# Gated linear attention and a cosine-gated MLP in one kernel: another form of the first two pairs' scores, and a new order of loads and steps

## The chip, the cores and the metric

One core of a Trainium2 chip. The metric is the device time of one execution in microseconds, the median of the runs that are shown.

## The reference

Attention with a decaying state for 4 batches, 8 heads, 768 tokens, head size 48, and then an MLP on the tokens:

```python
for t in range(S):
    state = alpha[:, :, t, :, None] * state + k_t[:, :, :, None] * v_t[:, :, None, :]
    y[:, :, t] = einsum('bhd,bhde->bhe', q[:, :, t], state)
x = y.transpose(0, 2, 1, 3).reshape(B * S, H * D)      # 3072 x 384
h = x @ w_in                                           # 384 x 2048
out = (h * cos(h)) @ w_out                             # 2048 x 384, float32
```

## The kernel before, in words

The tokens are worked on in twelve *pairs* J = 0 to 11 of 256 tokens, three pairs to a batch. A pair lies on 128 partitions with two tokens each (e = 0 for the even, 1 for the odd token) and is made of two chunks c of 64 partitions, 128 tokens each. For each pair there are these steps, each a small function:

- `load` (L107) brings a (alpha), k, q and v of a pair with one DMA each, 384 KB, on SP's queue. `load_w1` (L125) and `load_w2` (L131) bring quarters of the two weights with a cast to bf16 on GpSimd's queue, four of each.
- `ln` (L144) takes the logarithm of alpha on ScalarE; `cums0` and `cums` (L191, L173) sum the logarithms along the tokens with products against triangular matrices; for pairs from 3 on GpSimd first multiplies the two tokens' alphas (`mula`, L152) and VectorE subtracts (`sub`, L197). `icp` and `exps` (L206, L213) take exponentials on ScalarE; from pair 3 on they come together with the next logarithm as one `session` (L223, called "eb" in the plan). The exponential and the sine need different tables of ScalarE, which `act_set` (L139) and the activation load when they change.
- `scale_k`, `scale_q` (L231, L236; "sk", "sq") multiply k and q by the exponentials, on GpSimd or VectorE as the plan says. `cast_v` (L241) casts v on GpSimd.
- `trans` (L283) transposes k and q with TensorE and `evict_T` (L302) copies the result out; from pair 8 on a DMA does it (`trans_dma`).
- `scores` (L308) makes the products of k and q of a chunk, 128 x 128 for each head, 8 matmuls for each c. Its rows are the keys of the whole chunk (both tokens), its columns the queries. `mask` (L317) multiplies them by a triangular mask on VectorE.
- The v that meets these scores must have the chunk's 128 keys on 128 partitions. `stack_v` (L244; "vst") brings it there with four DMAs, and for pairs 0 to 2 `stack_v_pe` (L253; "vpe") does it with products against an identity, and `evict_vs` ("vev") copies the result out on ScalarE.
- `outer` (L324), `add_state` and `decay_state` (L351) carry the state from chunk to chunk; `decay` makes its factor. `yT` (L358) makes the output of the attention, transposed: from the state and q (12 or 24 matmuls), and from v and the masked scores (32 matmuls); `evict_y` (L386) copies it out to `xT`.
- `mlp1` (L396; "m1 u") makes a quarter of the first stage for a pair, 12 matmuls of 256 columns; `cosine` (L405) takes the cosine on ScalarE, as a sine with a shift; `gate` (L410) multiplies on VectorE. `mlp2` (L420; "m2 c part") makes a quarter of the second stage for 128 tokens, 4 matmuls of 384 columns; `evict_o` and `store` bring the result out.

Products into PSUM share three buffers of two banks each (tag "h": sums of the first pairs, transposes, scores, state products, y, first stage); a new one waits until the oldest user is copied out.

The order of all this is written out by hand: `PLAN` (L476) has for each step a row with one number for each pair, and the steps are issued in the order of these numbers, each engine working its instructions off in that order (":D" and ":A" behind a number put a step on VectorE or ScalarE). `IDLE` (L546) puts products of zeros, whose result nobody reads (`idle`, L454), between the steps. `GATES` (L99) holds loads back: a load that it names waits on SP until the last matmul of the step named there is done (`pass_gate`, L102). Before the change, the loads of pair 3 and a of pair 4 wait for the first pair's m2, c = 0, part 3; in the plan that stands after the loads of pair 2's a and q, which are not held back.

## Time and profile before

| | |
|---|---|
| median of 3 runs | 183.55 us (183.15 to 183.85) |
| the profiled execution | 183.31 us |
| its span, first to last instruction | 181.5 us |
| TensorE busy | 172.4 us (95%) |
| VectorE busy | 129.4 us (71%) |
| ScalarE busy | 123.9 us (68%) |
| GpSimd busy | 82.5 us (45%) |
| HBM read and written | 25.17 and 4.72 MB |
| granted TensorE clock | 1.00 |

PE is TensorE, PEld its weight loads, DVE VectorE, ACT ScalarE, POOL GpSimd; SPq and POOLq are DMA issues of SP and GpSimd. A row of a timeline has the start and the length in us, the engine, the line, the operation, result and sources, how many in a row, and in brackets how long the engine stood idle before it and who ended that. A strip has 40 digits, one for each 4.54 us, in tenths of busy time. In the DMA rows q1 is the queue of SP's loads and q0 that of GpSimd's weights: packets, MB, and the time of the packets as a share of 16 engines (above 100% where packets overlap).

### The profile page before, as it was taken

How to read it: one execution, taken by the hardware profiler on the slowest of the kernel's cores; microseconds unless marked ns; L12 is line 12 of the kernel's file. 1: busy time of each engine (PE TensorE's matmuls, PEld its weight loads, DVE VectorE, ACT ScalarE, POOL GpSimd, SP SyncE). 2: the span in 40 equal slices, each digit the busy share in tenths (PEclk: the TensorE clock that was granted, in tenths of full speed). 3: DMA queues.
4: the chain of work that ended last, by engine and by line, in shares of the span. 5: the costliest groups of instructions: out<-in, count | busy, mean ns of one | idle time of the engine just before them, and what ended most of it. 6: DMA issues, size and time to landing. Idle time of an engine off the chain costs nothing.

```text
span 181.5 us, 5505 instructions
## 1 busy us (share of the span) xinstructions
PE 172.4 (95%) x2339; PEld 123.6 (68%) x2342; DVE 129.4 (71%) x174; ACT 123.9 (68%) x159; POOL 82.5 (45%) x115
## 2 busy tenths in 40 slices
PE   7898789899999999999999999999999999999993
PEld 2444668665786767866786787778667767766672
DVE  7057976299989779699879898786877873535520
ACT  2765758988798999985688988937497704363201
POOL 6289770437486465959980495409025310000000
PEclk9999999999999999999999999999999999999999
DMA  5999999999969959984994998961669761030222
GB/s 143 261 261 250 153 192 202 247 251 269 236 151 285 263 123 297 276 214 105 298 180 79 269 121 219 185 144 33 131 147 262 89 154 68 2 130 4 87 87 87
DMA packets 68840, 31.55 MB, mean 174 GB/s; under 512 B 59728, under 2 KB 68816, under 8 KB 68816
## 3 DMA queue, kind: packets, MB, share of 16 engines
q1 hardware_dynamic: 64960, 27.96, 68.4%
q0 software_dynamic: 3712, 3.15, 11.6%
q8 instruction: 18, 0.29, 0.7%
q10 hardware_dynamic: 144, 0.10, 0.2%
q14 instruction: 6, 0.05, 0.1%
HBM read 25.17 MB, written 4.72 MB: 165 GB/s over the span
## 4 chain that ended last, share of the span: by engine, by line
PE 70%; DMA 9%; ACT 5%; POOL 4%; SPq 3%; issue 3%; DVE 3%; ACTq 0%
PE o_ps L431 28%; PE h_ps L401 28%; DMA w<-in_moe_w_out_dram 6%; PE y_ps L381 5%; SPq L110 3%; DMA v<-in_v_dram 3%; PE A_ps L314 3%; PE U_ps L332 2%; PE o_last L431 1%; DVE A_sb L320 1%; ACT L141 1%; POOL un L354 1%; POOL w L132 1%; PE T_ps L290 1%; ACT lna L146 1%
## 5 line engine op out<-in xcount | busy, mean ns | idle before, releaser
L413 DVE TENSOR_TENSOR gsb<-h_ps,c_sb 128x1024 bf16<-128x1024 f32 x48 | 57.9, 1222 | 23.0 <-ACT c_sb L408 22.1
L401 PE MATMUL h_ps<-xT,w 128*128 128x256 bf16 x576 | 68.5, 273 | 1.3 <-DVE A_sb L320 0.8
L431 PE MATMUL o_ps<-w,gsb 128*128 128x384 bf16 x368 | 67.0, 326 | 0.8 <-DMA w<-in_moe_w_out_dram 0.8
L408 ACT ACTIVATE c_sb<-h_ps,halfpi 128x1024 bf16<-128x1024 f32 x48 | 52.8, 1114 | 20.8 <-PE h_ps L401 20.6
L401 PEld LDWEIGHTS <-w 128*128 128x128 bf16 x576 | 55.2, 98 | 11.3 <-DMA w<-in_moe_w_in_dram 1.9
L431 PEld LDWEIGHTS <-gsb 128*128 128x128 bf16 x400 | 37.0, 98 | 21.9 <-issue 1.4
L320 DVE TENSOR_TENSOR A_sb<-A_ps,msk 128x1024 bf16<-128x1024 f32 x24 | 29.0, 1218 | 4.4 <-PE A_ps L314 4.2
L354 POOL TENSOR_TENSOR un<-us,c 128x384 bf16<-128x384 f32 x20 | 16.8, 838 | 31.5 <-DVE us L346 24.3
L233 POOL TENSOR_TENSOR kh<-k,icp 128x384 bf16<-128x384 f32 x19 | 19.7, 1038 | 9.1 <-ACT icp L209 5.2
L238 POOL TENSOR_TENSOR qh<-q,cp 128x384 bf16<-128x384 f32 x17 | 17.2, 1024 | 13.0 <-ACT cp L219 10.0
L390 ACT CAST xT<-y_ps 128x384 bf16<-128x384 f32 x12 | 6.7, 594 | 11.4 <-PE y_ps L381 11.3
L444 ACT COPY o_sb<-o_ps 128x384 f32<-128x384 f32 x12 | 5.7, 479 | 11.3 <-PE o_ps L431 11.3
L242 POOL CAST vp<-v 128x768 bf16<-128x768 f32 x12 | 10.1, 845 | 6.0 <-DMA v<-in_v_dram 5.7
L146 ACT ACTIVATE lna<-a 128x768 bf16<-128x768 f32 x12 | 10.1, 843 | 3.2 <-DMA a<-in_alpha_dram 3.2
L458 PE MATMUL idle_ps<-zeros 128*128 128x512 bf16 x38 | 10.8, 426 | 1.5 <-DVE halfpi L77 1.2
L141 ACT ACT_TABLE_LOAD x9 | 11.5, 1283 | 0.9 <-PEq L576 0.7
L408 ACT ACT_TABLE_LOAD x9 | 11.5, 1283 | 0.2
L154 POOL TENSOR_TENSOR a<-a 128x384 f32<-128x384 f32 x9 | 9.0, 1001 | 5.6 <-DMA a<-in_alpha_dram 5.6
L346 DVE TENSOR_TENSOR us<-U_ps,un 128x384 f32<-128x384 f32 x16 | 8.8, 551 | 2.6 <-PE U_ps L332 1.3
L444 DVE COPY o_sb<-o_ps 128x384 f32<-128x384 f32 x11 | 6.1, 555 | 4.8 <-PE o_ps L431 4.7
L314 PE MATMUL A_ps<-qkT 48*128 48x128 bf16 x192 | 8.8, 217 | 0.3 <-issue 0.3
L390 DVE CAST xT<-y_ps 128x384 bf16<-128x384 f32 x12 | 6.6, 586 | 2.1 <-PE y_ps L381 1.9
(68 smaller groups left out, 144.0 us busy)
## 6 DMA issues: line engine op xcount, KB each, us to landing
a<-in_alpha_dram SPq DMA_DIRECT2D x12, 384.0 KB, 5.8
k<-in_k_dram SPq DMA_DIRECT2D x12, 384.0 KB, 5.8
q<-in_q_dram SPq DMA_DIRECT2D x12, 384.0 KB, 6.0
v<-in_v_dram SPq DMA_DIRECT2D x12, 384.0 KB, 5.3
out_dram<-o_sb SPq DMA_DIRECT2D x23, 192.0 KB, 2.2
vs<-vp SPq DMA_DIRECT2D x36, 64.0 KB, 3.1
w<-in_moe_w_in_dram POOLq DMA_DIRECT2D x4, 384.0 KB, 7.0
w<-in_moe_w_out_dram POOLq DMA_DIRECT2D x4, 384.0 KB, 8.6
```

The lines of the kernel that those rows point to most:

```text
L141: nc.scalar.preload_act_table_set("natural_log_exp_and_others")
L146: nc.scalar.activation(out=lna_t[J % NL][:, :, :, 0:D].rearrange("p e h d -> p h e d"), in_=a_sb.pop(J), func=AF.Ln)
L233: eng.tensor_tensor(out=kh_t[J % NQ][:, :, e, :, 0:D], in0=kqv["k", J][:, :, e].rearrange("p (n a) d -> p n a d", a=2), in1=icp_.rearrange ...
L238: eng.tensor_tensor(out=qh_t[J % NQ][:, :, e, :, 0:D], in0=kqv["q", J][:, :, e].rearrange("p (n a) d -> p n a d", a=2), in1=cp.rearrange(" ...
L314: last = nc.tensor.matmul(A_ps[J, c][:, a, p, :], qkT[r, c, NP + p, :], qkT[r, c, p, :], start=True, stop=True)
L320: nc.vector.tensor_tensor(out=A_sb[J][:, c].rearrange("s a p t -> s (a p) t"), in0=A_ps.pop((J, c)).rearrange("s a p t -> s (a p) t"), in1 ...
L354: nc.gpsimd.tensor_tensor(out=u, in0=U_sum.pop(n), in1=c2_sb[J][:, :, c].unsqueeze(3).to_broadcast([C, NP, 2, D]), op=ALU.mult)
L390: ins = copy(out=xT[J][:, :, c * C : (c + 1) * C].rearrange("r i (t e) -> r i e t", e=2), in_=y_ps[J][:, c, 0 : KT * C].rearrange("r (i e ...
L401: last = nc.tensor.matmul(h_ps[J, u][:, f, :], w1[:, kk, ft * C : (ft + 1) * C], xT[J][:, kk, :], start=(kk == 0), stop=(kk == KT - 1))
L408: nc.scalar.activation(out=c_sb[J, u], in_=h_ps[J, u], func=AF.Sin, bias=halfpi, scale=1.0)
L413: nc.vector.tensor_tensor(out=gsb[J][:, u * FW : (u + 1) * FW], in0=h_ps.pop((J, u)), in1=c_sb.pop((J, u)), op=ALU.mult)
L431: last = nc.tensor.matmul(o[:, 0 : cols.stop - cols.start], gsb[J][:, ft, c * C : (c + 1) * C], w2[:, ft, cols], start=(done == 1 and ft = ...
```

## The change

- **Scores by parity of the key, for pairs 0 and 1** (`ALT`). The scores of a pair are split by the key's token e instead of by chunk: each product gives 64 rows, the keys of one token of one chunk, and the two chunks lie below each other on the partitions. 16 matmuls for each e instead of 8 for each c. Their rows lie as v lies anyway, so `yT` takes v unstacked, with 64 matmuls of 64 rows instead of 32 of 128. A mask `msk2` of its own is made at the start with eight more copies on VectorE.
- The unstacking of v for pairs 0 and 1 (steps "vpe" and "vev") is gone.
- **Gate:** a, k, q and v of pair 2 wait for the second quarter of pair 1's first stage ("m1 1", u = 1); the loads of pairs 3 and 4 are no longer held back.
- **Plan:** a new order of all steps. At the start: a, k, q, v of pair 0, then a, v, k, q of pair 1 (before: both a first, and q and a of pair 2 directly behind pair 1). The four w1 loads stand directly behind the first steps of pair 0. All scalings of q, and two of three of k, of pairs 0 and 1 go to VectorE. 27 idle products instead of 41.
- `WSPAN`, through which a weight load could cover several quarters, is empty, so each load covers one quarter as before.

```diff
+    ALT = (0, 1)
+    msk2 = consts.tile([C, 2, 2, HC], BF, tag="msk2")
+    for c in range(2):
+        r = slice(HC * c, HC * c + HC)
+        for e in range(2):
+            for e2 in range(2):
+                nc.vector.tensor_copy(out=msk2[r, e, e2], in_=(triu if e <= e2 else striu)[r, r])
...
-    GATES, AFTER = {('a', 3): ('m2', 0, 0, 3), ('k', 3): ('m2', 0, 0, 3), ('q', 3): ('m2', 0, 0, 3), ('v', 3): ('m2', 0, 0, 3), ('a', 4): ('m2', 0, 0, 3)}, {}
+    GATES, AFTER = {('a', 2): ('m1', 1, 1), ('k', 2): ('m1', 1, 1), ('q', 2): ('m1', 1, 1), ('v', 2): ('m1', 1, 1)}, {}
...
+    def scores_alt(J, e):
+        qkT = qkT_sb[J]
+        A_ps[J, e] = ps.tile([C, 2, NP, C], FP, tag="h", name="A_ps", bufs=3)
+        for p in range(NP):
+            for c in range(2):
+                for a in range(2):
+                    r = slice(64 * a, 64 * a + D)
+                    last = nc.tensor.matmul(A_ps[J, e][HC * c : HC * c + HC, a, p, :], qkT[r, c, NP + p, HC * e : HC * e + HC],
+                                            qkT[r, c, p, :], start=True, stop=True)
+        pass_gate(("scores", J, e), last)
...
-            in1=msk.rearrange("s e2 t -> s (e2 t)").unsqueeze(1).to_broadcast([C, H, C]), op=ALU.mult)
+            in1=(msk2[:, c] if J in ALT else msk).rearrange("s e2 t -> s (e2 t)").unsqueeze(1).to_broadcast([C, H, C]), op=ALU.mult)
...
+            for half, e, c in [(z // 4, z // 2 % 2, z % 2) for z in range(8)] if J in ALT else [(z % 2, 0, z // 2) for z in range(4)]:
...
+                        if J in ALT:
+                            r = slice(HC * c, HC * c + HC)
+                            todo.append((c, g, i, vp_t[J % NV][r, e].rearrange("s h d -> s (h d)")[:, m], A[r, e, a, p, :]))
```

The plan, for pairs 0 to 3 of the rows that the prediction speaks of (a smaller number is issued earlier):

```diff
-        "load a": "20 10 630 980 ...    "load k": "110 240 1160 1450 ...
-        "load q": "140 390 490 1530 ... "load v": "150 340 1200 1560 ...
-        "w1": "480 380 580 560 ...      "w2": "1080 1010 1090 860 ...
-        "ln": "50 30 640 1250 ...       "trans": "230 500 1270 1590 ...
-        "m1 0": "780 990 ...  "m1 1": "720 1130 ...  "m1 2": "840 930 ...  "m1 3": "810 1040 ...
-    IDLE = [(35, 10), (55, 3), (225, 9), (265, 5), (315, 6), (405, 4), (495, 3), (605, 1)]
+        "load a": "10 150 950 1100 ...  "load k": "50 310 990 1470 ...
+        "load q": "80 350 1130 1500 ... "load v": "120 190 1290 1650 ...
+        "w1": "300 270 370 410 ...      "w2": "980 630 940 840 ...
+        "ln": "20 320 960 1150 ...      "trans": "170 550 1260 1560 ...
+        "m1 0": "690 810 ...  "m1 1": "590 790 ...  "m1 2": "860 890 ...  "m1 3": "750 920 ...
+    IDLE = [(25, 10), (165, 8), (205, 1), (245, 1), (325, 1), (455, 6)]
```

In the new order the steps between the loads of pair 1 and the third pair's logarithm are: scores and mask of pair 0, y of pair 0 with both copies out on ScalarE, state products and transposes of pair 1, first quarter product (pair 0, u = 1), scores and masks of pair 1, second (0, 0), y of pair 1, third (0, 3), fourth (1, 1), then (1, 0), (0, 2), (1, 2), (1, 3), the second stage of pair 0, and sums, scalings and transposes of pair 2.

## The prediction, made before the changed kernel ran

> **What bounds the kernel now.** I read the strip of the span first, then the chain that ended last, then the timelines of the engines up to 50 us, then the DMA queues by window.

> ```profile
> PE   7898789899999999999999999999999999999993
> ```

> A digit is 4.54 us. From the eleventh digit on (45 us) TensorE is full to the end, so nothing after that can be gained except by less work for it. Before that it has holes, partly filled with idle products (L458).

> ```profile
> 25.55 10.58 DMA w<-in_moe_w_out_dram
> ...
> 41.65 0.32 PE cums L168
> ...
> 67.55 0.45 PE U_ps L332 x16
> 68.00 0.47 PE T_ps L290 x32
> 68.46 2.06 PE o_ps L431 x12
> 70.52 0.90 PE y_ps L381 x56
> ```

> The chain (start, us, what) runs through the weights' DMA until 36 us; after the sums of the fourth pair (41.65 + 0.32 = 41.97) it is almost only TensorE. I take **41.97 us as the mark**: by then TensorE has done all eight first-stage products of the first two pairs, the first pair's second stage, the third pair's sums and transposes and the fourth pair's sums. When the changed kernel has done the same set, the same work is left, and the time changes by the shift of the mark, plus what is given back behind it.

> ```profile
> 21.14 1.47 PE L401 MATMUL h_ps<-xT,w 128*128 128x256 bf16 x12 [0.75 <-DVE A_sb L320]
> ...
> 36.82 1.47 PE L401 MATMUL h_ps<-xT,w 128*128 128x256 bf16 x12
> ```

> The eight products of 12 matmuls run from 21.14 to 38.1; one takes 1.31 us (1.47 with its latency of 0.16). Back to back they would take 10.5 us, not 17. They wait for weights, for scores and for each other's buffers. That is the room for a gain: about 6 us at most.

> **The change part by part.** *Inputs.* The order on SP becomes a, k, q, v of pair 0, then a, v, k, q of pair 1.

> ```profile
> 4.53 0.84 ACT L146 ACTIVATE lna<-a 128x768 bf16<-128x768 f32 x1 [2.51 <-DMA a<-in_alpha_dram]
> 6.04 0.84 ACT L146 ACTIVATE lna<-a 128x768 bf16<-128x768 f32 x1 [0.66 <-DMA a<-in_alpha_dram]
> ```
> ```profile
> 13.59 0.82 POOL L242 CAST vp<-v 128x768 bf16<-128x768 f32 x1 [0.25 <-DMA v<-in_v_dram]
> 14.35 0.93 POOL L126 DMA_DIRECT2D w<-in_moe_w_in_dram  x1
> ```

> The first load lands at 4.53, the second at 6.04, the seventh (this v) at 13.5: 1.5 us each. So in the new order k of pair 1 (seventh) lands at 13.5 and its q (eighth) at 15.05. Eight loads, not ten, stand ahead of the weights.

> *Weights.* In the program as built the first w1 issue stands on GpSimd behind the cast of v0 and one small decay. v0 (fourth) lands at 9.05, the cast takes 0.8 to 1.1, so the issue is at about 10.4 instead of 14.35; the other three follow one state update, from 12.2 to 14.6. Do they slow k and q of pair 1, still under way? The two queues, packets, MB and share, in the windows 16.5 to 17.0, 17.5 to 18.0, 21.5 to 22.0 and 33.8 to 34.0:

> ```profile
> q1 hardware_dynamic: 322, 0.12, 111.2%
> q0 software_dynamic: 9, 0.01, 10.9%
> ...
> q0 software_dynamic: 92, 0.09, 113.1%
> q1 hardware_dynamic: 20, 0.01, 8.0%
> ...
> q0 software_dynamic: 31, 0.03, 101.1%
> ...
> q0 software_dynamic: 41, 0.03, 97.7%
> q1 hardware_dynamic: 40, 0.02, 28.3%
> ```

> The first weight, issued at 14.35, moves almost nothing until the inputs (q1) are through at 17; then it has the engines to itself. I read that as: what came first is finished first. Then q of pair 1 is undisturbed, and the weights begin at 14.3 instead of 17. The last window, inputs arriving as the last weights end, shows equal packet counts; that is rival A. A w1 load has 384 packets, at 92 in half a microsecond 2.1 us; four end by 23 (27 before), four w2 loads by about 31 (36.13 before).

> *The first two pairs.* Unstacking v takes two groups of products and two ScalarE casts away; scores by parity double the score matmuls (16 to 32 a pair) and the v part of y (32 to 64). At 0.90/56 = 16 ns each that is 96 x 16 = 1.5 us more for TensorE, bounded by nothing (if it fills holes) and 1.5; it lies before the mark, where TensorE waits anyway, and I count only what stands in the chain below. The eight mask copies added on VectorE fall before 6 us, when it has nothing to do until the first exponentials; price nothing.

> *The chain in the new order.* VectorE now scales q and k of pair 1, all three behind the mask of pair 0. Rows of VectorE:

> ```profile
> 16.32 1.02 DVE L238 TENSOR_TENSOR qh<-q,cp 128x384 bf16<-128x384 f32 x2
> ...
> 35.22 3.49 DVE L413 TENSOR_TENSOR gsb<-h_ps,c_sb 128x1024 bf16<-128x1024 f32 x3 [4.16 <-ACT c_sb L408]
> ...
> 40.91 1.28 DVE L305 COPY qkT<-T_ps 128x1024 bf16<-128x1024 bf16 x2
> ...
> 43.01 0.56 DVE L346 TENSOR_TENSOR us<-U_ps,un 128x384 f32<-128x384 f32 x1 [0.29 <-PE A_ps L314]
> 43.48 1.22 DVE L320 TENSOR_TENSOR A_sb<-A_ps,msk 128x1024 bf16<-128x1024 f32 x1
> 44.61 0.95 DVE L233 TENSOR_TENSOR kh<-k,icp 128x384 bf16<-128x384 f32 x1
> ```

> - k at 13.5, its scaling 0.55 and the mask 1.2: 15.3, when q is there.
> - three scalings: 0.51 each (16.32 row) to 0.95 (44.61 row), 1.5 to 2.85; I take 2.0, since a cast and a state update run on GpSimd beside the first two: 17.3.
> - outer product 0.45 and transposes 0.47 with latency: 18.3. The first product of the first stage follows at once (21.14 before).
> - two evictions, both on VectorE now, 1.28, and a state sum 0.55: 20.15; the first mask 1.2: **21.35**. In the built program the second product waits for exactly this mask, which frees its bank.
> - that product 1.31; y of pair 1 with 24 + 64 matmuls at 16 ns 1.4; a third product 1.31: 25.4. The fourth is the gate of the third pair's inputs: it ends at 26.7. Then four more at 1.31 (VectorE's gates go by 3.49/3 = 1.16, so TensorE sets the pace): **31.95**.

> ```profile
> 31.50 0.87 ACT L219 ACTIVATE cp<-cums_h 128x392 f32<-128x392 f32 x2
> ...
> 38.33 1.11 ACT L408 ACTIVATE c_sb<-h_ps,halfpi 128x1024 bf16<-128x1024 f32 x1 [0.76 <-PE h_ps L401]
> 39.46 1.28 ACT L141 ACT_TABLE_LOAD   x1
> 40.76 0.84 ACT L146 ACTIVATE lna<-a 128x768 bf16<-128x768 f32 x1
> ```

> - last sine 0.15 + 1.11, table load 1.28, logarithm 0.84: 35.35; sums 0.5 (one is 0.32), four exponentials at 0.44: 37.6; four scalings at 0.51 on VectorE (bound 0.95): 39.65; transposes 0.45: **40.1**. Before, the third pair's logarithm ran under the first products; now it stands behind the last sine and this stretch is exposed. TensorE has the second stage of pair 0 beside it, 32 matmuls at 2.06/12: 5.5 us, and the sums, and waits about 1.

> *The gate.* The waiting load stands on SP, and everything later on SP waits behind it, so the third pair's a starts at 26.8 at the earliest. It finds the weights still under way and lands when they are through, at 32 to 33.5; k, a of pair 3, q and v follow at 1.5. a is needed at 34.5 and q at 37.6, so the gate costs nothing; without that cover it would cost what is late at the logarithm. The traffic up to the fifth pair's a is the same set of loads in both programs.

> **Sum.** 40.1 - 41.97 = -1.9 us. Given back: in the built order the eviction of the third pair's y on ScalarE stands behind the exponentials of pair 4 and a logarithm (four at 0.44 and 0.84, 2.6 us); I find TensorE waiting 0.6 there, between nothing and 1.2. Net **-1.3 us**. The profiled execution took 183.31 us (span 181.5); that gives 182.0. The median of the three runs is 183.55, 0.24 above, so I say **182.1**. The bounds (1.5 to 2.85 for the scalings of pair 1, up to 1.75 more for those of pair 2, 0 to 1.2 given back) reach from 180.9 to 185.2; the upper ends are counted as C and D.

> **Rivals.**

> *A: the queues alternate packet by packet* (slower). From the moment the first weight has descriptors ready, about 12.8, until q of pair 1 is through, each input packet waits for a weight packet. A pair of packets takes 0.5/92 + 0.5/322 us over the engines (first and second window), so the 1024 rows of a load take 7.2 us instead of 1.5 and q lands near 20.7. The three scalings, the transposes and every product behind them stand in TensorE's order, so the chain moves by 5.7 less the 0.25 that q waits for VectorE now: mark 45.5, 187.4 us. It decides if the weights' packets start before 14 us. For it: 41 packets against 40 in the last window. Against: the second window, 92 against 20, and that nothing of the weight moved before 16.5. Chance 0.13.

> *B: the engines alternate by whole transfers.* Then q of pair 1 stands behind one weight, 2.1 us where the weight is ready before k is through (k's packets end near 12.7, the weight is ready at 12.5 to 13), so half of the engines or more; the last engine decides. Mark 41.95, 183.9 us: no change. The two windows fit it as well as the forecast. Chance 0.17.

> [...]

> *C: the exposed stretch is longer.* The weights' queue has a hole in this trace (31 packets in the window from 21.5, a third of 92); if it comes again and moves all loads behind it, or the scalings of pair 2 take 0.95 each as beside GpSimd's work, the third pair's transposes come 1 to 1.75 later: 183.1 to 183.9, no change. Chance 0.15.

> *D: the edit does less than it says:* the early products wait for scores and masks, not for weights, and the order is as long as the old one. The row at 21.14 names the mask, which speaks for it. It needs the chain up to 21.35 to be 2 us longer, by the scalings' upper bound and contention on every VectorE step: 184.0 to 185.3. Chance 0.07.

> **How the numbers follow.** Forecast 0.48, A 0.13, B 0.17, C 0.15, D 0.07. Half a per cent, 0.9 us, is about what a measurement of this kernel can tell from no change. Against the median the bounds of same are 182.6 and 184.5. The forecast case lies below them nine times in ten; B and C fall mostly within; A and D above. Faster 0.46 (with a little of C), same 0.28, slower 0.26 (with a third of B). The range 180.9 to 185.3 takes in all but A, and leaves out about 0.2 with the tails.

> **What would show it.** In the changed profile: q of pair 1 scaled on VectorE from about 15.3 (20 under A, 17 under B); the first products at 18.3 and 21.4; the eighth ending at 32; the third pair's logarithm at 34.5 directly behind a table load; its transposes ending at 40; TensorE full from about 49. Wrong would be: holes of TensorE later than 50 us, which this working takes to be none, or a third pair's a that lands after 34.5, which would make the gate the bound.

## The result and the profile after

| | before | after |
|---|---|---|
| median of 20 runs | 183.66 us (183.15 to 184.57) | 185.61 us (183.64 to 189.47) |
| the profiled execution, its span | 183.31, 181.5 us | 185.62, 183.7 us |
| granted TensorE clock | 1.00 in the profiled execution, 0.997 to 1.00 in all its runs beside the experiments | 0.997 to 1.00 in 9 of the 20 runs, 0.99 in 7, 0.98 in 4 |

The ratio is 1.0052, 95% interval 1.0029 to 1.0075: about half a per cent slower, not 0.8% faster. (It is made from undisturbed runs alone, those within 1.5% of the kernel's fastest, so it is smaller than the ratio of the medians.) The changed kernel also scatters over 6 us, the kernel before over 1.4, and its time goes with the clock: the median of the 9 runs at 0.997 to 1.00 is 184.3 us, of the 7 at 0.99 186.6, of the 4 at 0.98 188.0.

TensorE's strips of the changed kernel, busy time and granted clock, one digit for each 4.59 us:

```profile
PE   7885799889999999999599999999999999999993
...
PEclk9999999999999999999889999999999999999999
```

In the row of before every digit after the tenth was a 9, up to the last. Here the twentieth, 87 to 92 us, is a 5, and the granted clock drops in it and the next. From there to the end the row is as before.

The early chain first, TensorE and then ScalarE and VectorE (start, length, engine, line, operation, how many, and in brackets the idle time before and who ended it):

```profile
18.40 1.48 PE L428 MATMUL h_ps<-xT,w 128*128 128x256 bf16 x12
...
21.67 1.47 PE L428 MATMUL h_ps<-xT,w 128*128 128x256 bf16 x12 [0.87 <-DVE A_sb L344]
...
24.31 8.04 PE L428 MATMUL h_ps<-xT,w 128*128 128x256 bf16 x72
...
40.59 0.41 PE L300 MATMUL T_ps<-ident_bf,qh 64*128 64x64 bf16 x16 [0.69 <-DVE qh L248]
```
```profile
15.68 1.32 DVE L248 TENSOR_TENSOR qh<-q,cp 128x384 bf16<-128x384 f32 x2
16.92 0.55 DVE L243 TENSOR_TENSOR kh<-k,icp 128x384 bf16<-128x384 f32 x1
...
34.81 0.84 ACT L156 ACTIVATE lna<-a 128x768 bf16<-128x768 f32 x1
...
37.90 0.56 DVE L248 TENSOR_TENSOR qh<-q,cp 128x384 bf16<-128x384 f32 x1 [3.15 <-ACT cp L229]
...
38.38 1.04 DVE L243 TENSOR_TENSOR kh<-k,icp 128x384 bf16<-128x384 f32 x2
...
39.34 1.19 DVE L248 TENSOR_TENSOR qh<-q,cp 128x384 bf16<-128x384 f32 x1
```

The third pair's transposes make room for the next product at 40.59 + 0.33 = 40.92, where the prediction had 40.1 and the kernel before needed until 41.97 for the same work. So at the mark the changed kernel is 1.05 us ahead. At the end of the span it is 2.2 behind (183.7 against 181.5). Between lies this *hole*, a stretch in which TensorE stands idle, again in its timeline:

```profile
86.58 0.34 PE L408 MATMUL y_ps<-qkT,un 128*32 128x128 bf16 x12
86.74 0.50 PE L408 MATMUL y_ps<-A_sb,vs 128*32 128x128 bf16 x20
89.18 0.41 PE L408 MATMUL y_ps<-A_sb,vs 128*32 128x128 bf16 x12 [1.94 <-issue]
```

In the middle of y of pair 6, with 12 of its last 32 matmuls left, TensorE stops for 1.94 us. "issue" means that the profile shows nothing that it waits for. The chain of waits and the windows around it (TensorE's busy time is the second number of a window, the granted clock the third from the end) give the rest of the price:

```profile
71.54 4.04 PE h_ps L428 x36
...
87.24 1.94 issue
...
90.67 5.37 PE h_ps L428 x36
```
```profile
86.00:88.00 2.00, 1.24 (x88) 1.07 (x77) 1.41 (x3) 1.41 (x2) 1.67 (x2) 1.00 1.27 270
88.00:90.00 2.00, 0.82 (x28) 0.68 (x27) 0.37 (x1) 0.37 (x1) 2.00 (x4) 1.00 1.21 280
90.00:92.00 2.00, 2.00 (x19) 1.32 (x14) 2.00 (x3) 1.84 (x3) 1.77 (x3) 0.51 1.07 290
92.00:94.00 2.00, 2.00 (x13) 1.52 (x12) 0.54 (x1) 0.71 (x1) 1.16 (x2) 0.64 0.91 230
```

After the hole TensorE is granted half of its clock for 3.4 us (0.50 in the window 90.04 to 93.45; called a half clock below): the two windows lack (0.49 + 0.36) x 2 = 1.7 us of clock, at half rate that is twice as long. The 36 first-stage matmuls in it take 5.37 us, not 4.04. Hole and half clock cost 1.94 + 1.33 = 3.27 us; without them this execution would have taken about 182.3 (an estimate).

**What TensorE waits for.** The profile's page has a queue that moves no data of the kernel:

```profile
PE 171.8 (94%) x2414; PEld 124.1 (68%) x2416; DVE 129.8 (71%) x181; ACT 122.7 (67%) x160; POOL 77.7 (42%) x111
...
q8 instruction: 19, 0.31, 0.7%
```

```profile
q1 hardware_dynamic: 1399, 0.53, 126.4%
...
q1 hardware_dynamic: 1368, 0.52, 121.3%
q8 instruction: 1, 0.02, 3.8%
...
q1 hardware_dynamic: 135, 0.05, 124.7%
q8 instruction: 1, 0.02, 37.6%
```

One block moves from 86.3, for 3.8% of 2 us x 16 engines = 1.2 us, in a time in which the loads (q1) fill all engines. It is through at 87.5, after TensorE stopped (87.24), and TensorE goes on 1.6 us later. From this come two theories:

- **F:** TensorE ran out of instructions. The block came late, behind input loads, and the block in use was eaten quickly, because between 84 and 87 us stand the smallest matmuls of the kernel (transposes, y of two pairs): counted 256 recorded instructions back from the stop, it lasted from 84.1 to 87.2, 3.1 us. That a block is asked for about when the one before it is begun is the author's estimate; the trace shows only when its packet moves, here 2.2 us after that. The change left TensorE's work there as it was; it moved the block boundaries and the loads.
- **V:** TensorE waits there for data, the stacked v of pair 6 before all, whose four DMAs stand on SP between the loads.

### The profile page after: what moved, and what is told of

Read it like the earlier page. It is cut to its first block, busy times and chain, and to the rows that moved or that the text cites. A ratio compares the mean times of both kernels' runs of the same rounds, so it can differ in the third digit from the quotient of the medians.

```text
span 183.7 us, 5670 instructions
## 1 busy us (share of the span) xinstructions
PE 171.8 (94%) x2414; PEld 124.1 (68%) x2416; DVE 129.8 (71%) x181; ACT 122.7 (67%) x160; POOL 77.7 (42%) x111
## 4 chain that ended last, share of the span: by engine, by line
PE 84%; ACT 5%; DVE 4%; issue 2%; DMA 2%; POOL 1%; POOLq 0%
PE h_ps L428 35%; PE o_ps L458 31%; PE y_ps L408 5%; PE A_ps L338 3%; PE U_ps L356 3%; DMA a<-in_alpha_dram 2%; PE T_ps L300 2%; DVE qh L248 2%; PE o_last L458 1%; ACT icp L219 1%; DVE kh L243 1%; DVE A_sb L344 1%; PE cums L178 1%; ACT lna L156 1%; ACT cp L229 1%
## 5 line engine op out<-in xcount | busy, mean ns | idle before, releaser
L458 PE MATMUL o_ps<-w,gsb 128*128 128x384 bf16 x368 | 66.5, 326 | 0.0
L428 PEld LDWEIGHTS <-w 128*128 128x128 bf16 x576 | 56.2, 99 | 10.8 <-issue 1.0
L458 PEld LDWEIGHTS <-gsb 128*128 128x128 bf16 x400 | 36.8, 98 | 20.8
L248 POOL TENSOR_TENSOR qh<-q,cp 128x384 bf16<-128x384 f32 x16 | 15.9, 1004 | 9.8 <-DVE o_sb L471 6.6
L243 POOL TENSOR_TENSOR kh<-k,icp 128x384 bf16<-128x384 f32 x16 | 15.9, 1001 | 7.0 <-ACT icp L219 3.8
L471 ACT COPY o_sb<-o_ps 128x384 f32<-128x384 f32 x14 | 6.7, 477 | 14.5 <-PE o_ps L458 14.5
L417 ACT CAST xT<-y_ps 128x384 bf16<-128x384 f32 x14 | 7.7, 592 | 9.8 <-PE y_ps L408 9.6
L417 DVE CAST xT<-y_ps 128x384 bf16<-128x384 f32 x10 | 5.7, 587 | 5.4 <-PE y_ps L408 5.4
L485 PE MATMUL idle_ps<-zeros 128*128 128x512 bf16 x25 | 8.0, 463 | 1.3 <-DVE halfpi L84 1.2
L408 PE MATMUL y_ps<-A_sb,vs 128*32 128x128 bf16 x320 | 6.5, 219 | 1.9 <-issue 1.9
L248 DVE TENSOR_TENSOR qh<-q,cp 128x384 bf16<-128x384 f32 x8 | 5.6, 733 | 3.7 <-ACT cp L229 3.7
```

Source lines behind the costliest of these rows:

```text
L243: eng.tensor_tensor(out=kh_t[J % NQ][:, :, e, :, 0:D], in0=kqv["k", J][:, :, e].rearrange("p (n a) d -> p n a d", a=2), in1=icp_.rearrange ...
L248: eng.tensor_tensor(out=qh_t[J % NQ][:, :, e, :, 0:D], in0=kqv["q", J][:, :, e].rearrange("p (n a) d -> p n a d", a=2), in1=cp.rearrange(" ...
L408: last = nc.tensor.matmul(y_ps[J][32 * g : 32 * g + 32, c, i * C : (i + 1) * C], l, r, start=(c, g) not in begun, stop=(c, g, i) not in ou ...
L417: ins = copy(out=xT[J][:, :, c * C : (c + 1) * C].rearrange("r i (t e) -> r i e t", e=2), in_=y_ps[J][:, c, 0 : KT * C].rearrange("r (i e ...
L428: last = nc.tensor.matmul(h_ps[J, u][:, f, :], w1[:, kk, ft * C : (ft + 1) * C], xT[J][:, kk, :], start=(kk == 0), stop=(kk == KT - 1))
L458: last = nc.tensor.matmul(o[:, 0 : cols.stop - cols.start], gsb[J][:, ft, c * C : (c + 1) * C], w2[:, ft, cols], start=(done == 1 and ft = ...
```

## The experiments

Tiny products are matmuls of 2 columns on zeros, each one weight load and one matmul, put first on TensorE. They change nothing in the program but the number of instructions ahead of everything else:

```diff
+    def tiny(n):
+        ...
+            nc.tensor.matmul(idle_ps[0][:, 0:2], zeros[:, 0:C], zeros[:, 0:2], start=True, stop=True)
...
+    order.append((5, len(order), "tiny", [40]))
```

**Forty of them** (e1), and the same kernel again on another chip (e10).

> The changed kernel with 40 tiny products (128 x 2 columns, result unread) put first on TensorE, where it waits for the first inputs anyway. They move the places where TensorE's instruction stream passes from one 16 KB block to the next by 80 instructions. Theory F (the hole of 1.94 us at 87 us is TensorE waiting for its next block of instructions, whose transfer stands behind input loads; the half clock after it follows from the hole): the block that ran out at 87 us now begins at about 86.6 and was asked for at about 81.2, when the loads move little, so no hole from 50 us to the end, granted clock 1.00, and 185.62 - 1.94 - 1.7 = 182.0 us (181.5 to 182.6). Rival V (TensorE waits there for the stacked v of pair 6 or other data): the hole stays at the same product, 184 to 187.5 us.

> The changed kernel with the 40 tiny products again, beside the others of this call: 183.0 to 183.4 us median and granted clock 0.997 to 1.00 in nearly all runs, 0.3 to 0.5% under the kernel before. If that earlier gain was chance, no difference from the kernel before or from the changed kernel.

e1: 183.28 us against 183.95, ratio 0.995 (0.9924 to 0.9975), its profiled execution 182.02. e10: 182.79 against 183.61, ratio 0.9965 (0.9941 to 0.9989). Granted clock 0.997 to 1.00 in 22 of the 24 runs. The medians lie 0.8 to 1.3 us above F's 182.0, which only the fastest runs met, the profiled one of e1 among them; the hole is gone in both profiles. TensorE in e10:

```profile
87.53 0.34 PE L408 MATMUL y_ps<-qkT,un 128*32 128x128 bf16 x12
87.70 0.62 PE L408 MATMUL y_ps<-A_sb,vs 128*32 128x128 bf16 x32
88.25 0.62 PE L338 MATMUL A_ps<-qkT 48*128 48x128 bf16 x16
```

The 32 matmuls run through. One detail of the expectation was wrong: the block's packet still moves late (at 84.2 in e10, 83.4 in e1), beside full engines. What helps is that the block before it now begins 80 instructions further ahead, among longer matmuls, and lasts 5.2 us. In e10 the packet is through at 85.4 and its first instruction runs at 87.4, 2.0 us later, where the changed kernel needed 1.6; so little is to spare.

**138 of them in place of the first ten idle products** (e12): 256 instructions more, so by the estimate of 256 to a block the old boundaries are back.

> The changed kernel with 138 tiny products in place of the first ten idle products: 128 products more in all, 256 instructions, which is one block of 16 KB; so from the third block on the same instructions begin a block as in the changed kernel. F: the hole comes back in front of the last 12 products of y of pair 6, where with 40 tiny products it is gone: 184 to 189 us, granted clock 0.98 to 1.00. If tiny products help in another way (a warm engine, other times of the early steps), the time is that with 40 of them or better, 182 to 183.5 us, and no hole.

```profile
90.69 0.34 PE L408 MATMUL y_ps<-qkT,un 128*32 128x128 bf16 x12
90.86 0.50 PE L408 MATMUL y_ps<-A_sb,vs 128*32 128x128 bf16 x20
93.37 0.41 PE L408 MATMUL y_ps<-A_sb,vs 128*32 128x128 bf16 x12 [2.01 <-issue]
```

The hole is back at the same product: 186.58 us against 183.26, ratio 1.0159 (1.011 to 1.0209). Part of that is an early loss of its own (q of pair 1 landed at 17.9 us, so the first product of the first stage stands at 21.0, not 18.4). The place of the hole is what tells, not the time.

**The kernel before, with 54 tiny products** (e3).

> The kernel before with 54 tiny products at the start (108 instructions) and nothing else. F: one block is then used up between 88.5 and 90.5 us (y of two pairs and transposes), while the loads move 314 GB/s; the block after it, whose transfer needs about 2.5 us of waiting, 1.2 of its own and 1.6 until TensorE goes on, is 3 to 4 us late: a hole at about 90.5 us, half clock behind it in many runs, 186.5 to 189.5 us. V: products in an idle time change nothing, 183.4 to 183.9 us.

```profile
92.33 0.36 PE L290 MATMUL T_ps<-ident_bf,qh 64*128 64x64 bf16 x13
96.12 0.28 PE L290 MATMUL T_ps<-ident_bf,qh 64*128 64x64 bf16 x3 [3.42 <-issue]
96.34 4.83 PE L401 MATMUL h_ps<-xT,w 128*128 128x256 bf16 x29
```

A kernel without the change gets a hole from nothing but shifted boundaries, in front of a transpose, which needs no stacked v. 185.56 us against 183.95, ratio 1.0076 (1.0049 to 1.0102), less than F's 186.5 to 189.5, since three of the four runs kept the full clock; the profiled execution, with a half clock behind the hole, took 190.57. Of TensorE's recorded instructions (matmuls, weight loads, semaphore instructions) 2749 stand ahead of the hole here and 2751 in the changed kernel: the same place in the stream, but for the few records that a trace loses (the pages of the changed kernel and of e11, the same program, count 4830 and 4832), and other work. In e12 it is 3006, one block (255, a record being lost) later.

**The loads moved away, TensorE's instructions unchanged.** First by the plan alone (e4), then by the gate (e5):

```diff
e4  "load k", pair 9: 3220 -> 3521; "load q", pair 8: 3310 -> 3522; "load a", pair 10: 3430 -> 3523
e5  ('v', 7), ('k', 9), ('q', 8), ('a', 10): ('scores', 6, 1) added to GATES; their numbers 3341 to 3344
```

> The changed kernel with three loads (q of pair 8, k of pair 9, a of pair 10, issued between 81.5 and 86 us) moved in the plan behind y of pair 6; TensorE's instructions are the same, one by one. F: the block of instructions asked for at about 83.5 stands behind v of pair 7 and k of pair 8 alone, whose transfers end near 84.2, so it is there at about 87: hole 0 to 0.4 us, 182.0 to 182.8 us. V (stacked v): its four transfers were issued ahead of all these loads, so the hole stays, 184 to 187 us.

> The changed kernel, TensorE's instructions one by one the same, but four loads (v of pair 7, k of 9, q of 8, a of 10) wait for the scores of pair 6, which end near 83.9 us; only k of pair 8 goes ahead of them. Theory F: the block of instructions asked for at 83.5 to 84 finds the DMA engines nearly empty, starts at once (not 2.8 us later), and is there at about 86.5, ahead of the product that needs it at 87.0: no hole at 87, clock 1.00, 182.0 us as with the tiny products; 181.8 to 184 with the scatter of the early stretch. V: the hole stays, 184 to 188.

e4 tests nothing: SP's order came out as it was, since nothing else of SP lies between the old and the new numbers, and a plan number holds no load back in time. It is a second profile of the changed kernel, with the hole before the same 12 matmuls (1.46 us), 187.35 us against 183.95, ratio 1.018 (1.0146 to 1.0214). e5 does move them. Its DMA queues from 84 to 86 us, GB/s in 40 slices and the rows of the queues, and TensorE:

```profile
GB/s 208 108 92 23 0 0 0 0 0 0 0 0 0 0 0 0 0 0 0 0 0 0 0 0 328 0 0 0 0 0 0 0 0 84 77 100 138 92 108 138
...
q1 hardware_dynamic: 164, 0.06, 13.8%
q8 instruction: 1, 0.02, 3.5%
```
```profile
49.85 0.22 PE L192 MATMUL cums<-inchunk,lna 128*128 128x2 bf16 x3
50.47 0.16 PE L192 MATMUL cums<-inchunk,lna 128*128 128x2 bf16 x1 [0.41 <-issue]
...
87.28 0.34 PE L408 MATMUL y_ps<-qkT,un 128*32 128x128 bf16 x12
87.45 0.83 PE L408 MATMUL y_ps<-A_sb,vs 128*32 128x128 bf16 x32
```

The lone block is the 328 in the empty stretch: it moves at 85.2, 0.4 us after the block before it begins, and y of pair 6 runs through with the same instructions that stopped in the changed kernel. The small hole at 50.47 has 1471 recorded instructions ahead of it, five blocks (5 x 256 = 1280) fewer than 2751: a boundary again, where loads are still dense. Time 183.42 us against 183.12, ratio 1.0005 (0.9967 to 1.0042): the hole is gone in its profile, but the time is no better than that of the kernel before: two of ten runs have a granted clock of 0.99, and three others without that need 184.0 to 184.6 us.

**Twelve tiny products** (e2), and the changed kernel once more (e11).

> The same with 12 tiny products, 24 instructions. F: the block still begins in the middle of the dense small products at 87 us and is used up in about 3.4 us, so the hole stays, but 12 products earlier: 24 of the last 32 products of y of pair 6 are left behind it, not 12; 184 to 188 us. V: the hole stays in front of the last 12 products; the same time.

> The changed kernel as it is, beside the others on one chip. F: runs between 184 and 189 us with granted clocks of 0.98 to 1.00, 1.5 to 3.5 us above the one with the tiny products; the profile has the hole before the last 12 products of y of pair 6, whenever the block's transfer begins later than about 84.2 us. V or chance: no difference from the one with the tiny products.

e2: 183.59 us against 183.95; 0.9935 (0.9904 to 0.9965). F expected the hole 12 products earlier, but in its one profile (182.73 us) there was none: the packet moved at 84.9, after a wait of 0.45 us, and landed 1.8 us before it was needed. Six of its ten runs have a clock of 0.99; whether the hole is in those isn't shown. e11: 185.05 against 183.61, ratio 1.0079 (1.0052 to 1.0107), the hole before the last 12 matmuls a third time, 1.74 us.

The profiled executions of e4 and e11 both show a mean clock of 0.991, but their half clock isn't behind the hole; it is early, at 43.1 us in e4 and at 17.9 in e11. Their strips of the clock:

```profile
PEclk9999999996999999999999999999999999999999
...
PEclk9999699999999999999999999999999999999999
```

So a mean clock of 0.99 does not tell of a late hole, and how much of the changed kernel's 2 us is the hole with a half clock behind it, and how much early half clocks, is not settled. The hole alone shows in the runs at full clock: a median of 184.3 us in the changed kernel, 183.25 (e1) and 182.7 (e10) with 40 tiny products. Tiny products don't keep half clocks away by themselves: e7 and e9 below, with 40 of them and other orders of the loads, have one or two in 9 of 22 runs.

**The parts of the early gain.** No gate (e6), an earlier gate (e7), the scores by chunk (e8), q of pair 2 ahead of a of pair 3 (e9):

```diff
e6  GATES, AFTER = {}, {}                         (with 40 tiny products)
e7  ('m1', 1, 1) -> ('m1', 0, 0) in GATES          (with 40 tiny products)
e8  ALT = (); "vpe" 435 645, "vev" 445:A 665:A     (no tiny products)
e9  "load q", pair 2: 1130 -> 1095; "cums" 3: 1265; "sub" 3: 1267   (with 40 tiny products)
```

> The changed kernel with the 40 tiny products and without the gate: a, k, q, v of pair 2 start behind q of pair 1. The prediction's account (what comes first is finished first, and the gain is that the weights come early): four loads of 1.5 us stand ahead of most of the weights, the first products wait for weights up to 6 us longer, as in the kernel before or worse: 184 to 188 us. Rival G (the gate is what costs: q of pair 2 lands at 38 to 39.7 us where it is needed at 37.9): without it the third pair is early, 181 to 182 us.

189.08 us against 183.12, ratio 1.0334 (1.0295 to 1.0373), more than expected and on that side; its profile has two half clocks, both before 52 us (mean clock 0.982). Its chain of waits shows a weight 15.6 us under way:

```profile
23.51 15.59 DMA w<-in_moe_w_out_dram
39.10 0.04 issue
39.14 2.12 PE o_ps L458 x12
```

> The changed kernel with the 40 tiny products and the gate at the second product (pair 0, u = 0; it ends at 23.1) instead of the fourth (27.1). If the DMA engines' throughput sets when q of pair 2 lands (weights and inputs end when all bytes are through), nothing changes: median 183.3 as with the tiny products alone (182.0 to 184.2). G (the gate's place sets it): q lands 2 to 4 us earlier and the third pair no longer waits for it in any run: median 182.0 to 182.4.

183.78 us, 1.0022 (0.9998 to 1.0047). q of pair 2 lands no earlier: issued at 31.2 it arrives at 39.55, issued at 32.1 (e4) at 39.64, issued at 32.65 (e5) at 38.82. That fits the engines' throughput setting it, not the gate's place. It isn't free, though: five of its ten runs have a clock of 0.98 or 0.99, and its ratio lies above those of e1 and e10 (0.995 and 0.9965). The chains of e7 and e4:

```profile
31.16 8.39 DMA q<-in_q_dram
```
```profile
32.14 7.50 DMA q<-in_q_dram
```

> The changed kernel with the scores of pairs 0 and 1 by chunk again (v stacked by products and two ScalarE casts, 96 matmuls fewer and 8 more); its block boundaries from 45 us on stand as with the 40 tiny products, so no hole late. Parity helps the early chain: the casts stand on ScalarE between the exponentials and y of pair 0 and take a PSUM buffer, the eighth product ends 0.5 to 2 us later than 32.2, 183 to 185 us. Parity does nothing or costs (its 1.5 us of products stand on the path): the eighth product ends at 31.5 to 32.2, 181.5 to 183 us.

183.55 us, 1.0004 (0.9975 to 1.0033). In its profile the last six products of the first stage stand, as the chain has them, at

```profile
26.29 8.18 PE h_ps L428 x72
```

where the changed kernel has them from 24.31. Most of these 2 us are a half clock that this execution had from 18.2 us (its chain has the first product with 2.65 us, that of e7 with 1.43). In e11 the changed kernel had one at nearly the same place, 17.9, and its chain is the one to compare:

```profile
25.84 7.98 PE h_ps L428 x72
```

So parity brings the early chain about 0.5 us forward. In the ratios to the kernel before (1.0004 here, 0.995 and 0.9965 with 40 tiny products on other chips) it is 0.4 to 0.5%; whether that is parity or the half clocks stays open.

> The changed kernel with the 40 tiny products, q of pair 2 loaded ahead of a of pair 3, and the fourth pair's sums behind the third pair's transposes in TensorE's order. If the scatter that is left without the hole comes from q of pair 2 (it landed at 38.8 to 39.7 us in three profiles, where it is needed at 37.9), it now lands 1.5 us earlier, before it is needed: median 182.0 to 182.6, scatter under 1.5 us. Rival: a of pair 3 takes its place as what comes late (its sums wait, the session of pair 3 is 1 us later): median 183 or more.

184.01 us, 1.0017 (0.9985 to 1.005). The idea fell: q was scaled at 38.1, almost when it was wanted, and the time is worse than with the 40 tiny products alone (e10, on the same chip). What the scatter of the early stretch is made of isn't settled.

## Why the prediction was wrong

**The step that failed** is "holes of TensorE later than 50 us, which this working takes to be none", and with it "When the changed kernel has done the same set, the same work is left". The same work was left, but not the same stream: a new number of instructions ahead moves the block boundaries behind it (the holes of e3, the changed kernel and e12 have 2749, 2751 and 3006 recorded instructions ahead of them). What stood in place of "none" is a hole of 1.5 to 1.9 us near 87 to 92 us in all three profiles of the changed kernel, in one of them with a half clock behind it that cost 1.3 us more; half clocks, early or late, are a second term that the sum did not have. F is shown by three edits that leave the kernel's own work alone: 256 instructions more keep the hole, 80 more take it away, and the kernel before gets one from 108 more. e5 shows the other half: with the same instructions and the loads out of the way there is no hole. V is out by e3 and by the changed kernel's own trace: the eight DMAs of stacked v for pairs 6 and 5 were issued from 74.8 to 80.0 us and landed within 5.4 us, by 85.4 at the latest, before the first product that reads them (86.1). e5 alone would not rule it out, since held-back loads would let these DMAs through as well. That the half clock follows from the hole can't be said as a rule: it did in the changed kernel's profile, e3 and e12, and didn't in e4 and e11; the last section has what was measured on it.

After 42 us the changed kernel's TensorE has no other idle time above 0.3 us, so of the 15 packets that moved from there on one came late. Its price adds up from the trace: 2.2 us until the packet moved, the 1.2 us of the packet and 1.6 until TensorE went on are 5.0 us from the start of the block before it, which lasted 3.1; the difference is the hole of 1.94 us at 89.18.

The other steps, one by one:

- **Inputs and weights.** "What came first is finished first" held: q of pair 1 is scaled at 15.68 (15.3 said; the mask ahead of it set that), the three scalings end at 17.47 (17.3), the first product stands at 18.40 (18.3). Rivals A and B fall by that row. In other executions it held less well: q of pair 1 landed at 15.0 here, but at 8.60 + 7.38 = 16.0 in e7, 16.1 in e10 and 17.9 in e12, so some luck is in the 18.40.
- **The chain to the eighth product**: 21.67 (21.35) and 32.2 (31.95), the logarithm of pair 2 at 34.81 (34.5). Right within about 0.3.
- **The scalings of pair 2** were mis-sized: 37.90 to 40.53 is 2.6 us, where four at 0.51 made 2.04; the last, from 39.34, took 1.19 beside a cast on GpSimd (0.82 from 39.29). That is one of rival C's two mechanisms at a third of its price (0.6 of 1.75 us), and most of the 0.8 us between 40.1 and 40.92.
- **The gate.** In this execution it was as said, barely. a of pair 2, issued at 27.1, landed 6.2 us later at 33.3 (32 to 33.5 said); a of pair 3, two loads behind it, was there for GpSimd at 36.35; and q of pair 2, issued at 31.9, landed 5.9 us later at 37.8, 0.1 before its scaling:

```profile
36.35 0.99 POOL L164 TENSOR_TENSOR a<-a 128x384 f32<-128x384 f32 x1 [12.85 <-DMA a<-in_alpha_dram]
```

  "It costs nothing" was too confident all the same: q of pair 2, needed at 37.9, came at 38.8 to 39.6 in the chains of e4, e5 and e7. Without the gate the kernel with 40 tiny products takes 6 us more than the kernel before (e6).
- **The give-back** of 0.6 isn't seen: from the end of the third pair's transposes, e10 needs 180.9 - 41.58 = 139.3 us of its span, before 181.5 - 41.97 = 139.5.
- **The sum.** Without the hole, in the kernel with 40 tiny products, the order gains 0.7 us (e1) and 0.8 us (e10) in the medians, and 1.3 and 0.7 in the profiled executions against that of before, where the forecast was 1.3. The sign was right for the early stretch; the time was not, because of a term that was set to nothing. The step from 182.0 to 182.1 is also loose: 0.24 added to 182.0 would be 182.2.

The changed kernel with 40 tiny products is faster than both kernels, by 0.35 to 0.5% against the kernel before.

## What to carry to other kernels

When a change alters the number of instructions of an engine that works many short ones, look for the idle time that the profile lists under "issue" and put it beside the packets of the instruction queue: a hole at the same place in the stream, in whatever work stood there, was here a block that came late. Count how long each block lasts (about 256 recorded instructions here, by the estimate above); in these runs blocks that lasted 2 to 4.5 us under full DMA engines ran dry (e3, the changed kernel, the small hole of e5), those of 5.2 us did not (e1, e10), nor one of 3.4 us whose packet waited only 0.45 us (e2), nor one of 4.5 us in the changed kernel (45.2 to 49.8 us, its packet beginning to move at 47.1). 80 instructions without work, put where the engine waits anyway, moved the boundary, and the hole was gone (e1, e10); with loads held back that nobody needed yet, the packet moved 0.4 us after the block before it began, not 2.2, and the hole was gone too (e5). And before a mean clock is put down to a hole, look where in the span the clock fell.

## What the runs showed of the hardware

- The queue q8 moved 18 packets in the kernel before, 19 in the changed kernel and 20 in e12, 16 KB each, 0.7% of the 16 DMA engines in the first two; by the count above that fits TensorE's instructions. By the trace's packet times the packet in question began to move 0.4 us (e5, loads at 13.8% of the engines from 84 to 86 us) to 2.9 us (e3, loads at 121.4% from 92 to 94 us) after the block before it was begun, took about 1.2 us (3.5 and 3.9% of those 2 us x 16 engines), and TensorE, where it had stopped for it, went on 1.3 to 1.7 us after it was through.
- The hole of 1.94 us of TensorE was followed by half the clock, granted for 3.4 us (0.51 and 0.64 in two windows); the holes of 1.46 and 1.74 us in e4 and e11 were not. The profiles with one such time show 0.99 as their mean clock (the changed kernel, e4, e8, e11), those with two 0.98 (e6, e12).
- In the two traces of the changed kernel and of the kernel before, the stretches of full clock last 85.33 and 92.16 us (before and behind the half clock) and 177.49 us, which are 25, 27 and 52 times 3.413 us, the length of the half clock; the first of them begins at 4.70 us in the one and at 4.20 in the other. Counted in steps of that length from there, the step with the hole had 1.47 us of TensorE's work and half the clock behind it. Steps with more work had full clock behind them: 1.84 us from 14.94 in the changed kernel, 1.91 us from 17.86 in the kernel before, and 2.10 us with the hole of e4. The step with the hole in the changed kernel, and the one in e4, TensorE's busy time second:

  ```profile
  86.63:90.04 3.41, 1.47 (x70) 1.12 (x56) 1.19 (x3) 1.19 (x3) 3.39 (x5) 1.00 1.21 274
  ```
  ```profile
  90.88:94.29 3.41, 2.10 (x42) 1.72 (x42) 1.66 (x3) 1.65 (x4) 3.19 (x6) 1.00 1.16 287
  ```

  In e11 the hole, from 88.64 to 90.38, fell across two steps, with 2.49 and 2.59 us of work. So in these three profiles, of the same TensorE work, the half clock came where the whole hole of 1.94 us fell into one step, and not where 1.3 us of it did (e4) or 1.0 (e11); what it hangs on beyond these cases is not shown.
